# The last twelve blocks' out-projection as seven products a pair of blocks

## The chip, the cores and the metric

One core of a Trainium2 chip runs the kernel. Its engines work side by side, each through a list of instructions of its own, and wait for each other by semaphores: TensorE (PE in the profile) multiplies matrices from SBUF into the eight banks of PSUM; VectorE (DVE), ScalarE (ACT) and GpSimd (POOL) do elementwise work; SyncE (SP) issues most transfers between the chip's memory and SBUF. The metric is device time in microseconds (us) for one execution, lower is better.

## What is computed

```python
# linear attention with decay, 4 batches x 8 heads x 768 positions x 64, in blocks
intra = (qb @ kb.T * Dmask) @ vb
inter = (qb * lam_pow) @ kv_state
out   = intra + inter
kv_state = lam_block * kv_state + (kb * rev_pow).T @ vb
# then a feed-forward layer on x = out as (3072, 512)
h = x @ w_in            # (3072, 512) @ (512, 2048)
g = h * cos(h)
return g @ w_out        # (3072, 2048) @ (2048, 512)
```

Inputs and output are fp32; the matrix products work on bf16 copies and add up in fp32.

## The kernel before

The 3072 tokens are 24 blocks of 128. Attention goes by pairs of blocks (`pr`, 0 to 11): load q, k and v, prepare them (scale and cast, on GpSimd except early on), transpose q and k (by a DMA on SP's queue from pair 3 on), scores, state update, values. Its result, transposed, is `xT`.

The feed-forward layer goes by tiles, `TILES`, of two or four blocks. For each of the 16 slices `f` of 128 of the 2048 hidden columns TensorE multiplies `xT` by `w_in` into one PSUM bank (`ps_h`, four matmuls, line 753), ScalarE takes the cosine (`cos`, line 759), and VectorE multiplies the two into `g` in bf16 (line 765; "gate" below). Then, block by block, 16 matmuls over the slices add up g @ w_out into one bank (`ps_f`, line 800), with 512 columns of `w_out_sb` each. ScalarE copies the bank to `o_sb` (line 816) and SP's queue stores it. A tile's out-projection is interleaved with the hidden layer of the next tile; the last tile's stands alone at the end. The very last block is cut into 384 and 128 columns.

The order of all this is not written out by hand. `Planner` holds a list of tasks, each with an engine, a duration, what it depends on and a priority, and numbers of buffers (`BUFS`) and of PSUM banks. It plays them through once at build time, and each engine's instructions are emitted in the order found. An engine works strictly in that order: one that waits holds up all that stands behind it.

Tiles 5, 6 and 7 of before are the last twelve blocks, 12 to 23.

Of the kernel before, what the change touches and what calls it, by code (L numbers as in the profile page):

```python
# [19 lines left out]
DMA_FROM = 6  # L20
TILES = [4, 2, 2, 2, 2, 4, 4, 4]
SPLIT = 5
# [22 lines left out]
class Task:  # L45


    def __init__(self, eng, dur, deps, emit, prio, get=None, lat=None, banks=0):
        self.eng, self.dur, self.deps, self.emit, self.prio = eng, dur, [d for d in deps if d], emit, prio
        self.get, self.banks, self.lat = get, banks, lat  # L50

        self.frees, self.bank_frees = None, None

        self.worth = 0.0
        self.many = False

        self.then = None
        self.bank = []
        self.start = self.end = None
        self.ins, self.clears, self.extra = None, [], []  # L60


class Planner:
# [14 lines left out]
    def order(self):  # L78
# [3 lines left out]
        only = {}  # L82
        todo = list(self.tasks)
        while todo:
            first = {}
            for t in todo:
# [5 lines left out]
                if t.banks:  # L92
# [61 lines left out]
def kernel(  # L154
# [85 lines left out]

    unit = [MM(n * P, 4 * KF) + MM(DM, KF * n) + ATT * n for n in TILES]
    begins = [sum(unit[:i]) for i in range(len(unit) + 1)]
# [173 lines left out]
    def add_scores(pr, part):  # L416
# [293 lines left out]
    def add_span_state(s_t, prio):  # L710
# [20 lines left out]
        Uo[1, 1] = pl.add("POOL", 0.61, [x], state_16, prio)  # L731
        u.bank_frees = [[x]]

    h_last, o_last = {}, {}
    hid, closing = [], None

    def add_ffn(i):
        nb, n0 = TILES[i], first[i]
        cols = nb * P
# [230 lines left out]
```

## Time and profile before

| | before |
|---|---|
| median of 3 runs | 202.44 us (202.31 to 202.58) |
| span of the profiled execution, first to last instruction | 200.7 us; its own time is given only as this span |
| TensorE busy | 192.9 us, 96% |
| VectorE, ScalarE, GpSimd busy | 112.1, 117.1, 64.9 us |
| granted TensorE clock | 1.000 |

How to read it: busy shares tell which engine has little slack; the chain of waits, followed back from the last instruction, tells whose work the span is made of. "Idle before, releaser" is how long an engine stood still ahead of an instruction and what ended that. Matmuls overlap in the array, so the mean length of one (379 ns for 512 columns) is longer than its share of a stream of them; the latter is what counts for time.

### The profile page before, as it was taken

How to read it: one execution, taken by the hardware profiler on the slowest of the kernel's cores; microseconds unless marked ns; L12 is line 12 of the kernel's file. 1: busy time of each engine (PE TensorE's matmuls, PEld its weight loads, DVE VectorE, ACT ScalarE, POOL GpSimd, SP SyncE). 2: the span in 40 equal slices, each digit the busy share in tenths (PEclk: the TensorE clock that was granted, in tenths of full speed). 3: DMA queues.
4: the chain of work that ended last, by engine and by line, in shares of the span. 5: the costliest groups of instructions: out<-in, count | busy, mean ns of one | idle time of the engine just before them, and what ended most of it. 6: DMA issues, size and time to landing. Idle time of an engine off the chain costs nothing.

```text
span 200.7 us, 5731 instructions
## 1 busy us (share of the span) xinstructions
PE 192.9 (96%) x2380; PEld 110.2 (55%) x2407; DVE 112.1 (56%) x211; ACT 117.1 (58%) x223; POOL 64.9 (32%) x86
## 2 busy tenths in 40 slices
PE   8899999999999999999999999999999999999993
PEld 2466444648758647858755454544445444444452
DVE  2978772448848816956745679565445453444001
ACT  5878771329769527939555878486356465344120
POOL 5893002284373645472636570006400000000000
DMA  5999999999899999998999997999611010111112
GB/s 163 303 191 202 205 196 239 289 221 177 203 218 214 184 241 201 214 213 184 191 207 220 245 206 183 318 314 223 162 56 54 3 52 6 49 52 52 52 63 97
DMA packets 96668, 34.46 MB, mean 172 GB/s; under 512 B 84738, under 2 KB 93186, under 8 KB 96642
## 3 DMA queue, kind: packets, MB, share of 16 engines
q1 hardware_dynamic: 89664, 29.83, 66.6%
q0 software_dynamic: 6832, 4.20, 14.5%
q8 instruction: 19, 0.31, 0.7%
q10 hardware_dynamic: 146, 0.07, 0.1%
q14 instruction: 7, 0.06, 0.1%
HBM read 27.26 MB, written 6.29 MB: 167 GB/s over the span
## 4 chain that ended last, share of the span: by engine, by line
PE 89%; DMA 6%; issue 1%; SPq 1%; POOL 1%; ACT 0%; POOLq 0%
PE ps_f L800 41%; PE ps_h L753 41%; DMA sp_f<-in_k_dram 3%; DMA w_in_sb<-in_moe_w_in_dram 3%; PE ps_o L491 2%; PE ps_o L523 2%; PE ps_kv L441 2%; PE ps_s L429 1%; SPq L260 1%; POOL k_sp L614 1%; PE ps_t L381 0%; PE ps_kv L718 0%; PE ps_x L491 0%; ACT o_sb L816 0%; POOLq L614 0%
## 5 line engine op out<-in xcount | busy, mean ns | idle before, releaser
L765 DVE TENSOR_TENSOR g<-ps_h,cos 128x256 bf16<-128x256 f32 (+1 forms) x133 | 70.6, 543 | 41.4 <-ACT cos L759 39.7
L800 PE MATMUL ps_f<-w_out_sb,g 128*128 128x512 bf16 (+2 forms) x380 | 87.6, 370 | 2.2 <-issue 1.6
L753 PE MATMUL ps_h<-xT,w_in_sb 128*128 128x256 bf16 (+1 forms) x525 | 88.8, 319 | 0.5 <-issue 0.2
L759 ACT ACTIVATE cos<-ps_h,halfpi 128x256 f32<-128x256 f32 (+1 forms) x133 | 72.0, 570 | 28.9 <-PE ps_h L753 28.3
L753 PEld LDWEIGHTS <-w_in_sb 128*128 128x128 bf16 x532 | 51.4, 98 | 32.9 <-DMA w_in_sb<-in_moe_w_in_dram 0.4
L800 PEld LDWEIGHTS <-g 128*128 128x128 bf16 x400 | 37.6, 98 | 40.4
L351 POOL TENSOR_TENSOR qk<-q_f,q_scale 128x512 bf16<-128x512 f32 x19 | 19.4, 1042 | 54.2 <-DMA q_f<-in_q_dram 54.2
L816 ACT COPY o_sb<-ps_f 128x512 f32<-128x512 f32 (+1 forms) x24 | 13.7, 574 | 22.6 <-PE ps_f L800 19.6
L359 POOL TENSOR_TENSOR v_s<-v_f,v_scale 128x512 bf16<-128x512 f32 x19 | 19.6, 1043 | 9.2 <-DMA v_f<-in_v_dram 5.4
L531 ACT CAST xT<-ps_o 128x512 bf16<-128x512 f32 x15 | 8.1, 589 | 13.6 <-PE ps_o L523 11.2
L434 DVE TENSOR_TENSOR s_m<-ps_s,mask 128x512 bf16<-128x512 f32 x20 | 12.9, 685 | 2.5 <-PE ps_s L429 2.0
L355 POOL CAST qk<-k_f 128x512 bf16<-128x512 f32 x18 | 11.0, 612 | 7.8 <-DMA k_f<-in_k_dram 7.8
L447 DVE TENSOR_TENSOR sum<-sum,ps_kv 128x512 f32<-128x512 f32 x15 | 10.2, 682 | 0.7
L451 ACT CAST S<-sum 128x512 bf16<-128x512 f32 x15 | 9.1, 618 | 1.0 <-DVE sum L447 0.9
L508 DVE COPY spare<-ps_o 1x1 f32<-1x1 f32 x8 | 1.2, 156 | 14.6 <-PE ps_o L491 14.6
L816 DVE COPY o_sb<-ps_f 128x384 f32<-128x384 f32 x1 | 0.6, 558 | 11.6 <-PE ps_f L800 11.6
L491 PEld LDWEIGHTS <-v_s 64*64 64x64 bf16 x320 | 4.2, 106 | 4.4 <-issue 4.0
L491 PE MATMUL ps_o<-s_m,v_s 64*64 64x64 bf16 x288 | 5.9, 197 | 0.0
L638 DVE TENSOR_TENSOR s_m_sp<-ps_s,mask_sp 128x512 bf16<-128x512 f32 x8 | 5.1, 685 | 1.3 <-PE ps_s L633 1.3
L892 PE MATMUL ps_idle<-const-float32-1.0 128*128 128x512 f32 (+1 forms) x6 | 4.8, 902 | 0.8 <-PEq L954 0.8
L523 PE MATMUL ps_o<-qkT,S 64*64 64x64 bf16 x304 | 5.0, 195 | 0.0
L441 PE MATMUL ps_kv<-v_s,qk 64*64 64x64 bf16 x288 | 4.8, 195 | 0.0
(77 smaller groups left out, 83.9 us busy)
## 6 DMA issues: line engine op xcount, KB each, us to landing
q_f<-in_q_dram SPq DMA_DIRECT2D x20, 256.0 KB, 3.9
k_f<-in_k_dram SPq DMA_DIRECT2D x20, 256.0 KB, 4.5
v_f<-in_v_dram SPq DMA_DIRECT2D x20, 256.0 KB, 4.5
out_dram<-o_sb SPq DMA_DIRECT2D x19, 256.0 KB, 2.8
w_out_sb<-in_moe_w_out_dram POOLq DMA_DIRECT2D x3, 512.0 KB, 13.6
sp_f<-in_q_dram SPq DMA_DIRECT2D x2, 512.0 KB, 4.9
sp_f<-in_k_dram SPq DMA_DIRECT2D x2, 512.0 KB, 5.4
w_in_sb<-in_moe_w_in_dram POOLq DMA_DIRECT2D x2, 512.0 KB, 9.1
```

The costliest lines, as they stand in the source:

```text
L351: return vec[e].tensor_mul(new_qk()[:, 0, :, s], live.pop(("q_f", 2 * pr + s)), q_scale[:, c, :].unsqueeze(2).to_broadcast([P, H, D]))
L355: return (nc.scalar.copy if early else nc.gpsimd.tensor_copy)(new_qk()[:, 1, :, s], live.pop(("k_f", 2 * pr + s)))
L359: return vec[e].tensor_mul(live["v_s", 2 * pr + s], live.pop(("v_f", 2 * pr + s)), v_scale[:, c, :].unsqueeze(2).to_broadcast([P, H, D]))
L434: return nc.vector.tensor_mul(t, live["s", pr][s], mask.unsqueeze(1).to_broadcast([P, H, D]))
L447: return nc.vector.tensor_add(new, live["sum", pr, 0] if half else live["sum", pr - 1, 1], live["kv", pr][half])
L451: return nc.scalar.copy(new_S(pr, half), live["sum", pr, half])
L491: yield lambda h=h: nc.tensor.matmul(o[halves[h % 2], h // 2], lhsT=live["v_s", n0 + s][m, h, :], rhs=live["s_m", n0 + s][m, h, :], start= ...
L753: return [nc.tensor.matmul(t[:, :n], lhsT=w_in_sb[:, kd, f * P:(f + 1) * P], rhs=live["xT", i][:, kd, at], start=(kd == 0), stop=(kd == KD ...
L759: nc.scalar.activation(c[:, :n], live["h", i, f, at.start][:, :n], AF.Sin, bias=halfpi)
L765: return nc.vector.tensor_mul(live["g", i][:, f, at], live.pop(("h", i, f, at.start))[:, :n], live.pop(("c", i, f, at.start))[:, :n])
L800: return [nc.tensor.matmul(live["f", i, j, piece][:, :width], lhsT=live["g", i][:, f, j * P:(j + 1) * P], rhs=w_out_sb[:, f, part], start= ...
L816: return (nc.scalar.copy if eng == "ACT" else nc.vector.tensor_copy)(o[:, :width], live["f", i, j, piece][:, :width])
```

## The change

A pair of blocks and the two halves of the 2048 hidden columns make `g` a matrix of two by two blocks, a11 to a22 (first index: block of the pair). `w_out` is cut likewise: b11 to b22 (first index: half of its rows; second: half of its 512 columns). Strassen's scheme takes seven products where the plain one takes eight:

- "5": (a11+a12) b22, "2": (a21+a22) b11, "1": (a11+a22)(b11+b22), "3": a11 (b12-b22), "4": a22 (b21-b11), "7": (a12-a22)(b21+b22), "6": (a21-a11)(b11+b12).

Each product is eight matmuls of 256 columns, in two groups `g` of four slices of rows. Three banks are taken by a pair: A for 5 and 2, B for 1, C for 3 and 4 and, added onto them later, 6 and 7 (the very last pair has a bank D as well). ScalarE copies A to `SA`; VectorE makes `E` = B - SA in two halves, `o1` = C + SA (two quarters of the result), and, once 7 and 6 have been added onto C, `o2` = C + E (the other two). Products 7 and 6 wait until o1 has read C.

The sums on g's side are VectorE's, five for each group of each tile: `cmb` for 5, 2 and 1, and in place in `g` for 7 and 6. The sums of `w_out` are made once: three on GpSimd, into three tiles that hold the first pairs' data until then ("wide"), each in four instructions placed behind the preparation of a v; two in place in `w_out_sb`, eight instructions of VectorE, after the last plain out-projection has read it.

```diff
-TILES = [4, 2, 2, 2, 2, 4, 4, 4]
+FAST = [5, 6, 7, 8]
+TILES = [4, 2, 2, 2, 2, 4, 2, 2, 4]
+WIDE = ["11+22", "12-22", "21-11"]
+ON = ["DDDDDDDDDD"] * 9
+SLOT = list(range(6, 18))
+WSUM = [("11+22", "POOL", 2, 70.0), ("12-22", "POOL", 2, 70.0), ("21-11", "POOL", 2, 70.0), ("21+22", "DVE", 2, 100.0), ("11+12", "DVE", 2, 100.0)]
+SEQ = [[(n, (g,)) for g, x in enumerate(("52341", "34521")) for n in x] + [(n, (0, 1)) for n in "76"], [(n, (0, 1)) for n in "5234176"]]
...
+                if t.lock:
+                    at = max(at, free.get("POOL", 0.0))
+                if t.eng == "POOL":
+                    at = max(at, locked)
...
-    BUFS = {"ld": 6, "qk": 3, "v_s": 6, "qkT": 3, "s_m": 4, "cos": 3, "o_sb": 3, "o_held": 12}
+    BUFS = {"ld": 4, "qk": 3, "v_s": 6, "qkT": 3, "s_m": 4, "cos": 3, "o_held": 13, "cmb": 6, "SA": 1, "E": 1}
...
+        def two(_, name, g, at, e):
+            f, z = slice(QF * g, QF * g + QF), slice(HF + QF * g, HF + QF * g + QF)
+            b = {"11": w_out_sb[:, f, low], "12": w_out_sb[:, f, high], "21": w_out_sb[:, z, low], "22": w_out_sb[:, z, high]}
+            v = nc.vector if e == "DVE" else nc.gpsimd
+            return (v.tensor_add if name[2] == "+" else v.tensor_sub)(place(name, g)[:, at], b[name[:2]][:, at], b[name[3:]][:, at])
...
+        slices = [[f] for x in range(HF) for f in (x, x + HF)] if nb == 4 else [[x, x + HF] for x in range(HF)]
...
+            def hidden(task, fs=fs):
+                t = live["h", i, fs[0]] = bank(task.bank[0], [P, len(fs), cols], F32, "ps_h")
...
+        def combine(_, name, g, e):
+            v = nc.vector if e == "DVE" else nc.gpsimd
+            a11, a12, a21, a22 = (side(x, y, g) for x in range(2) for y in range(2))
+            if name in "125":
+                c = live["cmb", i, name, g] = work.tile([P, QF, np_, P], BF16, tag="cmb", bufs=BUFS["cmb"], name="cmb")
+                return v.tensor_add(c, *{"5": (a11, a12), "2": (a21, a22), "1": (a11, a22)}[name])
+            if name == "7":
+                return v.tensor_sub(a12, a12, a22)
+            return v.tensor_sub(a21, a21, a11)
...
+                    def product(task, name=name, g=g, p=p, to=to, half=half, what=what, opens=opens):
+                        if opens:
+                            live["f", i, p, to] = bank(task.bank[0], [P, 2, HM], F32, "ps_f")
+                        t = live["f", i, p, to][:, half]
+                        return [nc.tensor.matmul(t, lhsT=left(name, f, p), rhs=right(what, f),
+                                                 start=(f % QF == 0 and opens is not None), stop=(f == HF - 1), skip_group_check=True)
+                                for f in range(QF * g, QF * g + QF)]
...
+                        return nc.scalar.copy(live["SA", i, p], live["f", i, p, "A"])
...
+                        return nc.vector.tensor_sub(live["E", i, p][:, half], live["f", i, p, "B"][:, 0], live["SA", i, p][:, 1 - half])
...
+                        return nc.vector.tensor_add(o, live["f", i, p, "C"], live["SA", i, p])
...
+                nc.sync.dma_start(out=out[rows(0), high], in_=o[:, 0])
+                nc.sync.dma_start(out=out[rows(1), low], in_=o[:, 1])
...
+                    return nc.vector.tensor_add(o, live["f", i, p, "C"], e)
...
     def add_ffn(i):
+        if i in FAST:
+            return add_fast_ffn(i)
```

Up to the last plain out-projection (block 11) the order on TensorE, VectorE and ScalarE is as before. Below, lines are those of each kernel; old 765 is new 829 (gate), old 434 and 447 are new 452 and 465 (masked scores, state addition), old 508 is new 526 (a small marker copy). New are 776 (w_out sums), 850 (`cmb`), 852 and 853 (7 and 6 in place), 921 (E), 931 and 932 (o1), 958 and 959 (o2).

VectorE from the first gate of tile 5 on, before:

```order
L765 TENSOR_TENSOR g<-ps_h,cos 128x512 x9
L508 COPY spare<-ps_o 1x1
L765 TENSOR_TENSOR g<-ps_h,cos 128x512 x2
L434 TENSOR_TENSOR s_m<-ps_s,mask 128x512 x2
L447 TENSOR_TENSOR sum_2788<-sum_2502,ps_kv 128x512
L765 TENSOR_TENSOR g<-ps_h,cos 128x512 x2
L447 TENSOR_TENSOR sum_2812<-sum_2788,ps_kv 128x512
```

and now, from the masked scores of that tile on:

```order
L452 TENSOR_TENSOR s_m<-ps_s,mask 128x512 x2
L850 TENSOR_TENSOR cmb<-g 128x1024
L829 TENSOR_TENSOR g<-ps_h,cos 128x512 x3
L850 TENSOR_TENSOR cmb<-g 128x1024
L829 TENSOR_TENSOR g<-ps_h,cos 128x512
L850 TENSOR_TENSOR cmb<-g 128x1024
L829 TENSOR_TENSOR g<-ps_h,cos 128x512
L852 TENSOR_TENSOR g<-g 128x8x128
L853 TENSOR_TENSOR g<-g 128x8x128
L829 TENSOR_TENSOR g<-ps_h,cos 128x2x256
L850 TENSOR_TENSOR cmb<-g 128x1024
L829 TENSOR_TENSOR g<-ps_h,cos 128x2x256
```

The sums of the first group stand between the tile's last gates, those of the second between the first gates of tile 6, and the two state additions have moved behind these and the first pair's o1 and E. Ahead of this piece the eight w_out sums (776) stand between the first eleven gates.

VectorE at the program's end, before:

```order
L434 TENSOR_TENSOR s_m<-ps_s,mask 128x512 x2
L447 TENSOR_TENSOR S_3342<-sum_3001,ps_kv 128x512
L765 TENSOR_TENSOR g<-ps_h,cos 128x512
L542 TENSOR_TENSOR xT<-ps_o,cross_3419 128x4x64
L542 TENSOR_TENSOR xT<-ps_o,cross_3425 128x4x64
L765 TENSOR_TENSOR g<-ps_h,cos 128x512 x16
L816 COPY o_sb<-ps_f 128x384
```

and now, from the last gates on:

```order
L829 TENSOR_TENSOR g<-ps_h,cos 128x512 x2
L850 TENSOR_TENSOR cmb<-g 128x1024 x3
L852 TENSOR_TENSOR g<-g 128x8x128
L853 TENSOR_TENSOR g<-g 128x8x128
L921 TENSOR_TENSOR E<-ps_f,SA 128x256 x2
L931 TENSOR_TENSOR o_sb<-ps_f,SA 128x512
L958 TENSOR_TENSOR o_sb<-ps_f,E 128x512
L932 TENSOR_TENSOR o_sb<-ps_f,SA 128x256 x2
L921 TENSOR_TENSOR E<-ps_f,SA 128x256 x2
L959 TENSOR_TENSOR o_sb<-ps_f,E 128x256 x2
```

Behind the last gate stand five sums of the second group, and then both pairs' E, o1 and o2; the last one ends the program with its store.

GpSimd in two pairs' preparation (351, 355, 359 are q, k, v; new 369, 373, 377), before:

```order
L351 TENSOR_TENSOR qk<-q_f,q_scale 128x8x64 x2
L355 CAST qk<-k_f 128x8x64 x2
L359 TENSOR_TENSOR v_s<-v_f,v_scale 128x512 x2
L351 TENSOR_TENSOR qk<-q_f,q_scale 128x8x64 x2
L355 CAST qk<-k_f 128x8x64 x2
L359 TENSOR_TENSOR v_s<-v_f,v_scale 128x512 x2
```

and now:

```order
L369 TENSOR_TENSOR qk<-q_f,q_scale 128x8x64 x2
L373 CAST qk<-k_f 128x8x64 x2
L377 TENSOR_TENSOR v_s<-v_f,v_scale 128x512
L776 TENSOR_TENSOR w_12-22_1486<-w_out_sb 128x512
L377 TENSOR_TENSOR v_s<-v_f,v_scale 128x512
L776 TENSOR_TENSOR w_12-22_1486<-w_out_sb 128x512
L369 TENSOR_TENSOR qk<-q_f,q_scale 128x8x64 x2
L373 CAST qk<-k_f 128x8x64 x2
```

A w_out sum now stands behind each v of six pairs, and so ahead of the next pair's q.

More of the change, by code (lines that the diff above doesn't have):

```diff
@@ L109, in order @@
             free[t.eng] = t.end
+            if t.lock:
+                locked = t.end
             only.pop(t.eng, None)
@@ L239 @@
     live = {}
-    unit = [MM(n * P, 4 * KF) + MM(DM, KF * n) + ATT * n for n in TILES]
+    HF, HM = KF // 2, DM // 2
+    QF = HF // 2
+    unit = [MM(n * P, 4 * KF) + (MM(HM, 7 * HF * n // 2) if i in FAST else MM(DM, KF * n)) + ATT * n for i, n in enumerate(TILES)]
     begins = [sum(unit[:i]) for i in range(len(unit) + 1)]
@@ L455, in add_scores @@
         for s in range(2):
-            So[n0 + s] = pl.add("DVE", 0.69, [s_t] + ([So[n0]] if s else []), partial(scores_out, s=s), pa(0.25 + 0.1 * s), get="s_m")
+            So[n0 + s] = pl.add("DVE", 0.69, [s_t] + ([So[n0]] if s else []), partial(scores_out, s=s), pa(0.25 + 0.1 * s) - (HASTE if pr >= 8 else 0.0), get="s_m")
         s_t.bank_frees = [[So[n0]], [So[n0 + 1]]]
@@ L597 @@
     spans, span_deps = [], []
-    span_v = [consts.tile([P, H, 2, D], BF16, name=f"v_sp{x}") for x in range(SPANS)]
+    span_s = [consts.tile([P, 2, NP, 2, P], BF16, tag="wide", bufs=3, name=f"s_m_sp{x}") for x in range(SPANS)]
+    span_vs = consts.tile([P, SPANS, H, 2, D], BF16, tag="wide", bufs=3, name="v_sp")
+    span_v = [span_vs[:, x] for x in range(SPANS)]
     def add_span(x):
@@ L732, in add_span_state, with add_w_sums, place @@
         u.bank_frees = [[x]]
+        wide_free.append(u)
     h_last, o_last = {}, {}
     hid, closing = [], None
+    W, w_sum, passed, closed = {}, {}, {}, [None]
+    low, high = slice(0, HM), slice(HM, DM)
+    DUR = {"gate": (0.6, 0.17), "cos": (0.59, 0.16), "copy": (0.47, 0.18), "half": (0.34, 0.17)}
+    def add_w_sums():
+        def place(name, g):
+            if name in WIDE:
+                if name not in W:
+                    W[name] = consts.tile([P, HF, HM], BF16, tag="wide", bufs=3, name=f"w_{name}")
+                return W[name][:, QF * g:QF * g + QF]
+            return w_out_sb[:, QF * g:QF * g + QF, high] if name == "11+12" else w_out_sb[:, HF + QF * g:HF + QF * g + QF, low]
+        def two(_, name, g, at, e):
[3 more added lines that the diff above has]
+            return (v.tensor_add if name[2] == "+" else v.tensor_sub)(place(name, g)[:, at], b[name[:2]][:, at], b[name[3:]][:, at])
+        slots = []
+        for k, (name, e, parts, prio) in enumerate(WSUM):
+            for g in range(2):
+                loaded = [w_t["out", 0], w_t["out", 2]] if g == 0 else [w_t["out", 1]] + w_last
+                w_sum[name, g] = []
+                for x in range(parts):
+                    at = slice(x * QF // parts, (x + 1) * QF // parts)
+                    slot = [d_t[SLOT[len(slots)]]] if len(slots) < len(SLOT) else []
+                    slots.append(1)
+                    t = pl.add(e, {"DVE": 0.07 + 0.55 / parts, "POOL": 2.08 / parts}[e], loaded + slot + (wide_free if name in WIDE else [closed[0]] + w_sum[{"11+12": "12-22", "21+22": "21-11"}[name], g]),
+                               partial(two, name=name, g=g, at=at, e=e), prio + k + 0.4 * g + 0.01 * x)
+                    t.lock = e == "DVE"
+                    w_sum[name, g].append(t)
@@ L785, in add_ffn @@
             last = n0 + j == NBLK - 1
-            tag = "o_held" if n0 + j < len(HELD) or i == len(TILES) - 1 else "o_sb"
+            tag = "o_held"
             cuts = [0, 3 * DM // 4, DM] if last else [0, DM]
```

152 lines of the change are left out of this document (150 added, 2 removed).

## The prediction, made before the changed kernel ran

> **What bounds the kernel now.** I read the page's head and chain first, then busy time by stage, the chain in order of time, the groups by shape, and the timelines of VectorE, GpSimd and the SP queue where the change puts work.
>
> ```profile
> span 200.7 us, 5731 instructions
> PE 192.9 (96%) x2380; PEld 110.2 (55%) x2407; DVE 112.1 (56%) x211; ACT 117.1 (58%) x223; POOL 64.9 (32%) x86
> PE 89%; DMA 6%; issue 1%; SPq 1%; POOL 1%; ACT 0%; POOLq 0%
> ```
>
> TensorE is the chain. The stages that change begin with the hidden layer of tile 5 (blocks 12 to 15), at 109.7 us. In the stages below (columns: stretch, length, then busy us and count of each engine, granted clock, DMA share, GB/s) the clock is full and TensorE is idle for 0.8 of 74.3 us, so what TensorE no longer does comes off the span, unless another engine makes it wait.
>
> ```profile
> 109.50:125.00 15.50, 15.39 (x192) 7.66 (x193) 11.93 (x20) 12.72 (x21) 6.57 (x8) 1.00 1.04 206
> 125.00:131.50 6.50, 6.34 (x153) 3.47 (x152) 3.92 (x8) 3.37 (x6) 0.00 (x0) 1.00 0.94 314
> 131.50:159.60 28.10, 27.68 (x294) 13.39 (x297) 14.07 (x23) 15.78 (x27) 5.31 (x6) 1.00 0.49 130
> 159.60:183.80 24.20, 24.09 (x111) 10.96 (x112) 10.38 (x15) 12.65 (x20) 0.00 (x0) 1.00 0.09 33
> ...
> 183.80:200.70 16.90, 13.76 (x79) 7.05 (x78) 1.25 (x2) 2.71 (x5) 0.00 (x0) 1.00 0.21 79
> ```
>
> VectorE, the third busy time, is 40.3 us there and almost idle after 183.8. It takes nearly all of the new work.
>
> **TensorE's work.** The chain in order of time gives the price of one matmul in a stream (start, length, what):
>
> ```profile
> 77.68 6.99 PE ps_h L753 x64
> 101.34 5.18 PE ps_f L800 x24
> 190.50 7.12 PE ps_f L800 x48
> 197.65 0.27 ACT o_sb L816
> ```
>
> The 64 of the first row are 256 columns wide: 109 ns each. The 24 of the second are 512 wide: 216 ns. In the third, 16 are 512 wide (3.45) and the last block's 16 of 384 and 16 of 128 take the other 3.67.
> - Removed: 11 blocks x 16 x 0.216 + 3.67 = 41.65 us of out-projection.
> - Added: 6 pairs x 7 products x 8 = 336 matmuls of 256 columns, each with its own weights as in the first row: 336 x 0.1092 = 36.69. Gain 4.96.
> - The split of the third last tile turns 64 matmuls of 512 into 128 of 256 in its hidden layer: 13.98 for 13.81, a loss of 0.17. Cosine and gate still work on 512 columns, since two slices share a bank, so their number stays.
>
> TensorE does 4.79 us less.
>
> **VectorE's prices.** Groups by shape, then pieces of its timeline (start, length, count, idle before):
>
> ```profile
> L765 DVE TENSOR_TENSOR g<-ps_h,cos 128x512 bf16<-128x512 f32 x59 | 40.5, 691 | 31.7 <-ACT cos L759 31.2
> L765 DVE TENSOR_TENSOR g<-ps_h,cos 128x256 bf16<-128x256 f32 x74 | 30.3, 424 | 9.8 <-ACT cos L759 8.5 <-DMA v_f<-in_v_dram 0.7
> L384 DVE COPY qkT<-ps_t 128x1024 bf16<-128x1024 bf16 x2 | 1.4, 692 | 3.3 <-PE ps_t L381 3.3
> ```
> ```profile
> 107.11 1.29 DVE L434 TENSOR_TENSOR s_m<-ps_s,mask 128x512 bf16<-128x512 f32 x2
> 117.34 0.69 DVE L765 TENSOR_TENSOR g<-ps_h,cos 128x512 bf16<-128x512 f32 x1 [0.17 <-ACT cos L759]
> 58.42 0.76 DVE L542 TENSOR_TENSOR xT<-ps_o,cross 128x256 bf16<-128x256 f32 x2 [1.33 <-ACT cross L548]
> ```
>
> (The last row's shape is that of the 424 ns form.) An instruction of 512 fp32 elements lasts 0.69, but two in a row end after 1.29: one costs 0.60 when work waits. Two of 256 end after 0.76: 0.34 each. Adding a PSUM product to an SBUF tile has these forms, so a pair's E (two halves), o1 and o2 cost 2 x 0.34 + 2 x 0.60 = 1.9; six pairs 11.3.
>
> Sums of bf16 with both inputs in SBUF don't occur in the trace. From the slope of the first two rows (267 ns for 256 elements), 1024 elements would last 0.691 + 2 x 0.267 = 1.23 at one element a step; the COPY moves 1024 bf16 elements in 0.692. I take the COPY's, the only row with the type and the number of elements: 0.60 in a stream for 1024 (tiles of four blocks), 0.34 for 512 (tiles of two, and the w_out sums); 1.13 and 0.60 are the other end. Added: 20 x 0.60 + 20 x 0.34 + 8 x 0.34 = 21.5. [...]
>
> In all 32.8 us join VectorE's 40.3, in a stretch of some 86: not the bound as a whole, but it can be late in places. I walked its new order against TensorE's there.
>
> *Hidden layer of tile 5.* VectorE idles 15.50 - 11.93 = 3.6 us, mostly in gaps of 0.17 ahead of a gate. Eight w_out sums (2.7) fit if they run at once. GpSimd reads SBUF meanwhile:
>
> ```profile
> 113.88 2.04 POOL L351 TENSOR_TENSOR qk<-q_f,q_scale 128x512 bf16<-128x512 f32 x2 [2.21 <-DMA q_f<-in_q_dram]
> 118.18 2.07 POOL L359 TENSOR_TENSOR v_s<-v_f,v_scale 128x512 bf16<-128x512 f32 x2 [0.39 <-DMA v_f<-in_v_dram]
> 136.22 2.04 POOL L351 TENSOR_TENSOR qk<-q_f,q_scale 128x512 bf16<-128x512 f32 x2 [15.97 <-DMA q_f<-in_q_dram]
> ```
>
> About five of the sums fall into 113.9 to 120.3. Whether they and GpSimd hold each other up no row shows: from nothing to five times its 1.04 us. I take half an instruction each, 2.6 us of VectorE, of which its gaps absorb most; at the attention pair (118.7 on), where banks of late gates are wanted, TensorE waits 0.4.
>
> *Tile 5's products.* Behind the gates come three sums, the last gates, 7 and 6, then the second half's five, with tile 6's gates between. By my walk the second half's 5 and 2 are done at 130.2 and 131.4; TensorE, at the old pace, wants them at 130.7 and 131.1. With the semaphore: 0.5. The two state additions (old L447), moved behind E and o1, have until the next attention pair, some 13 us on, and cost nothing; if they came later, that pair would wait for them and their cast, about 1.2 (two forms of 0.6).
>
> *Last tile.* Its start today (the out-projection's first matmul, the last cosine, the last gate):
>
> ```profile
> 183.60 14.02 PE L800 MATMUL ps_f<-w_out_sb,g 128*128 128x512 bf16 x79
> 183.80 0.69 ACT L759 ACTIVATE cos<-ps_h,halfpi 128x512 f32<-128x512 f32 x1 [0.28 <-PE ps_h L753]
> 184.52 0.69 DVE L765 TENSOR_TENSOR g<-ps_h,cos 128x512 bf16<-128x512 f32 x1 [1.03 <-ACT cos L759]
> ```
>
> The last gate ends 1.6 us after the last hidden matmul. Then five sums, E and o1 of its first pair (8 instructions, 4.3 us in a stream) must be done when TensorE gets to product 7 of that pair, 6.1 on: level at 0.60 each, 0.6 late at 0.69. I take 0.3.
>
> Waits together 1.2, with ends of 0 and, if single rate or blocking holds, some 7.
>
> **Other parts.** *End.* The last copy (0.27) becomes an addition of the 0.42 form, +0.15. Its store grows from 64 to 128 KB:
>
> ```profile
> out_dram<-o_sb SPq DMA_DIRECT2D x1, 192.0 KB, 1.9
> out_dram<-o_sb ACTq DMA_DIRECT2D x1, 64.0 KB, 1.6
> ```
>
> Between these, +0.15. Together +0.3 (0.15 to 0.45).
>
> *GpSimd's twelve sums* of 512 elements go two to a pair of blocks, ahead of the next pair's q. The nearest two-input row:
>
> ```profile
> L359 POOL TENSOR_TENSOR v_s<-v_f,v_scale 128x512 bf16<-128x512 f32 x19 | 19.6, 1043 | 9.2 <-DMA v_f<-in_v_dram 5.4 <-PE ps_h L753 2.4 <-PE ps_kv L441 0.9
> 79.73 1.04 POOL L359 TENSOR_TENSOR v_s<-v_f,v_scale 128x512 bf16<-128x512 f32 x1 [1.01 <-DMA v_f<-in_v_dram]
> 83.75 2.05 POOL L351 TENSOR_TENSOR qk<-q_f,q_scale 128x512 bf16<-128x512 f32 x2 [2.98 <-DMA q_f<-in_q_dram]
> ```
>
> 2.09 us go into a wait of 2.98 for the load of q: free. At 1.5 us or more each, the excess delays the next transposes on the SP queue and all loads behind them; without that cover, 2.1 a pair.
>
> *SP queue.* Up to the first store of tile 5 its order is unchanged. Four load buffers instead of six add no wait there: each pair's loads already stand behind transposes that wait for a later preparation. But loads of the last pair of blocks now stand among tile 5's stores:
>
> ```profile
> 131.41 1.72 SPq L260 DMA_DIRECT2D q_f<-in_q_dram  x2
> 133.18 2.90 SPq L260 DMA_DIRECT2D k_f<-in_k_dram  x2
> 140.50 2.68 SPq L387 DMA_TRANSPOSE qkT<-qk  x2
> 153.28 0.43 PE L429 MATMUL ps_s<-qkT 64*64 64x64 bf16 x32
> ```
>
> k goes from 133.2 to about 137.5, behind o2 of tile 5's first pair, and the transposes from 140.5 to about 145. The scores that need them come at 153: 6 us of cover; beyond it each us costs one. Each pair stores four pieces of 128 KB for two of 256, on a queue with little else left: free.
>
> *ScalarE* loses these copies and gains six of the form:
>
> ```profile
> L816 ACT COPY o_sb<-ps_f 128x512 f32<-128x512 f32 x12 | 7.0, 586 | 12.8 <-PE ps_f L800 9.8 <-remote 2.9
> ```
>
> It idles ahead of them today, so nothing is gained or lost. *PSUM*: a pair holds three banks where a block held one, so a late VectorE is felt sooner; this is in the 1.2.
>
> **Sum.** -4.96 + 0.17 + 1.2 + 0.3 = -3.3. The profiled execution spans 200.7, so 197.4 of span; the runs' median lies 1.74 above it (202.44), and I keep that: **199.1 us**. Case range 198.4 to 200.4 (waits of 0.5 to 2.5).
>
> **Rivals.**
> 1. *VectorE is never late:* no waits, the gain less the end: 202.44 - 4.79 + 0.3 = 198.0. For it: VectorE's gaps in every stage above. Against it: my walk, late at two places by tenths.
> 2. *VectorE's sums and GpSimd's reads exclude each other.* If a sum waits out a whole GpSimd instruction, the five cost 5.2 us, with a gate behind each; pair 11's preparation (136.2 on) hits tile 5's sums again. Beyond the gaps TensorE loses some 3 instead of 1.2: 201. [...]
> 3. *Slower: bf16 sums run at one element a step.* 20 x 0.53 + 28 x 0.26 = 18 us more of VectorE. In tile 5's products it then has 8 gates (4.8), attention (2.6), ten sums (11.3) and two pairs (3.7), 22.4, plus some 4 left over, against 21 of TensorE: 5 late; at the end 2.5 more. Waits 7.5: 205.4. It decides from waits of 4.5 on, a long sum of about 0.88 us in a stream. For it: every two-input row of the trace has that rate (all fp32); against it: the COPY.
>
> **Chances.** Forecast 0.55, rival 1 0.15, rival 2 0.15, rival 3 and what else delays TensorE by over 4.5 us 0.15. Range 197.7 (rival 1 with the shortest end and today's gaps gone) to 202.0 (rival 2's upper part), leaving out rival 3 and a little. A change of 0.2% (0.4 us) is about what this measurement can tell from none. Faster 0.82, same 0.04, slower 0.14.
>
> **What would show it.** Out-projection at 109 ns a matmul, 336 of them; 1024-element sums of 0.69 and 512-element ones near 0.42; TensorE idle about 1.2 us more than now, put down to VectorE, at tile 5's products and at the last tile; GpSimd's sums of 1.04 ending before q lands; the chain up to 109.7 as before. Wrong would be sums of 1.2, or stretched ones beside GpSimd; matmuls above 0.109; waits of the last attention pair for its transposes.

## The result and the profile after

Four runs of the changed kernel took 200.6 us in the median (199.5 to 200.86), the kernel before 202.51 beside them: a ratio of 0.990, 95% interval 0.987 to 0.992. It is faster by 1.9 us where 3.3 were forecast. The profiled execution took 200.86 us with a span of 199.2. Medians and ranges are of fast runs; one slow run of the kernel with 60 idle matmuls (203.53) and three of the kernel without the split are left out of theirs.

The head of its page, busy time, and the chain by engine:

```profile
span 199.2 us, 6216 instructions
PE 190.0 (95%) x2577; PEld 130.1 (65%) x2599; DVE 146.3 (73%) x284; ACT 113.7 (57%) x217; POOL 79.3 (40%) x98
PE 87%; DVE 7%; DMA 2%; issue 2%; ACT 1%; DVEq 0%
```

TensorE is still the chain, but VectorE, which had no part in it, now holds 7%, and "issue" went from 1% to 2%. The stages of before, from tile 5's first gates on (columns as in the prediction):

```profile
109.50:125.00 15.50, 14.46 (x188) 7.17 (x189) 14.74 (x25) 11.53 (x18) 7.37 (x8) 1.00 1.14 185
125.00:131.50 6.50, 6.50 (x59) 5.50 (x57) 6.50 (x12) 2.85 (x5) 0.00 (x0) 1.00 0.79 221
131.50:159.60 28.10, 26.34 (x454) 23.04 (x453) 24.62 (x48) 13.75 (x23) 6.12 (x6) 1.00 0.66 167
159.60:183.80 24.20, 24.04 (x215) 15.41 (x217) 20.91 (x41) 13.67 (x24) 0.00 (x0) 1.00 0.10 34
183.80:199.20 15.40, 12.16 (x112) 10.62 (x109) 8.74 (x17) 1.80 (x3) 0.00 (x0) 0.99 0.25 87
```

TensorE, idle for 0.8 us of the first four stretches before, is idle for 3.0 of them now. VectorE has hardly a gap up to 131.5. These are TensorE's four longest waits there, from its timeline (in brackets the idle time ahead of the row and what ended it):

```profile
121.19 4.49 PE L820 MATMUL ps_h<-xT,w_in_sb 128*128 128x512 bf16 x19 [0.93 <-DVE g L829]
132.20 0.61 PE L897 MATMUL ps_f<-w_out_sb,cmb 128*128 128x256 bf16 x4 [0.41 <-DVE cmb L850]
141.66 0.22 PE L541 MATMUL ps_o<-qkT,S 64*64 64x64 bf16 x2 [1.04 <-issue]
157.21 0.35 PE L459 MATMUL ps_kv<-v_s,qk 64*64 64x64 bf16 x11 [0.31 <-ACT SA L914]
```

The first is the hidden layer after tile 5's attention, waiting for a bank that a late gate holds. The second is the second half of product 2. The third stands inside an attention visit (the block of attention matmuls of one pair), 30 of its last 32 matmuls done, and no semaphore explains it. The fourth waits for a copy to SA that stands behind a cosine on ScalarE. The new instructions' groups (the last number is the mean in ns):

```profile
L850 DVE TENSOR_TENSOR cmb<-g 128x1024 bf16<-128x1024 bf16 x12 | 8.7, 753 | 0.1
L850 DVE TENSOR_TENSOR cmb<-g 128x512 bf16<-128x512 bf16 x12 | 5.2, 455 | 0.1
L776 DVE TENSOR_TENSOR w_out_sb<-w_out_sb 128x512 bf16<-128x512 bf16 x8 | 4.9, 634 | 0.0
L776 POOL TENSOR_TENSOR w_11+22_953<-w_out_sb 128x512 bf16<-128x512 bf16 x4 | 4.6, 1155 | 0.0
```

The same shape, 128x512, has a mean of 455 ns in one place and 634 in another. VectorE's and GpSimd's timelines show why:

```profile
114.57 0.41 DVE L776 TENSOR_TENSOR w_out_sb<-w_out_sb 128x512 bf16<-128x512 bf16 x1
119.35 1.05 DVE L776 TENSOR_TENSOR w_out_sb<-w_out_sb 128x512 bf16<-128x512 bf16 x1
120.44 1.29 DVE L829 TENSOR_TENSOR g<-ps_h,cos 128x512 bf16<-128x512 f32 x2
122.84 1.50 DVE L850 TENSOR_TENSOR cmb<-g 128x1024 bf16<-128x1024 bf16 x1
```
```profile
119.08 1.04 POOL L377 TENSOR_TENSOR v_s<-v_f,v_scale 128x512 bf16<-128x512 f32 x1 [0.15 <-POOL qk L373]
122.75 1.04 POOL L377 TENSOR_TENSOR v_s<-v_f,v_scale 128x512 bf16<-128x512 f32 x1 [2.63 <-DMA v_f<-in_v_dram]
```

A w_out sum takes 0.41 alone. The one that starts at 119.35, in the middle of GpSimd's v (119.08 to 120.12), ends at 120.40, 0.28 after GpSimd's end. The gate behind it ends at 121.13, and TensorE goes on at 121.19. The first sum of g, 0.68 elsewhere, does the same at 122.84 and ends 0.55 after GpSimd's v.

To compare kernels I divide the span at weight loads, all of which are in the trace (some matmul records are missing): what lies ahead of tile 5's first weights; then the time from each weight load to the next, summed over the feed-forward layer and over attention; and what follows the last one.

| us | before | changed | changed, again | quiet GpSimd | half on GpSimd | the same, again |
|---|---|---|---|---|---|---|
| ahead of tile 5 | 109.30 | 108.98 | 109.28 | 109.45 | 109.18 | 109.27 |
| feed-forward from there | 83.45 | 79.35 | 78.76 | 78.76 | 78.83 | 79.31 |
| attention from there | 4.59 | 7.25 | 6.93 | 5.81 | 5.42 | 6.38 |
| behind the last weights | 3.4 | 3.6 | 3.5 | 3.6 | 3.6 | 3.7 |
| span | 200.7 | 199.2 | 198.5 | 197.6 | 197.0 | 198.6 |

(The last four columns are experiments below.) The feed-forward layer gives 4.1 to 4.7 us, as forecast; attention, in which the change adds no work, takes 0.8 to 2.7 of it back.

### The profile page after: what moved, and what is told of

It is laid out like the page before. It is cut to its first block, busy times and chain, and to the rows that moved or that the text cites. A ratio compares the mean times of both kernels' runs of the same rounds, so it can differ in the third digit from the quotient of the medians.

```text
span 199.2 us, 6216 instructions
## 1 busy us (share of the span) xinstructions
PE 190.0 (95%) x2577; PEld 130.1 (65%) x2599; DVE 146.3 (73%) x284; ACT 113.7 (57%) x217; POOL 79.3 (40%) x98
## 4 chain that ended last, share of the span: by engine, by line
PE 87%; DVE 7%; DMA 2%; issue 2%; ACT 1%; DVEq 0%
PE ps_h L1001 21%; PE ps_f L1048 21%; PE ps_h L820 17%; PE ps_f L897 17%; DVE g L829 3%; DMA sp_f<-in_q_dram 2%; DVE cmb L850 2%; PE ps_o L509 2%; PE ps_t L642 1%; PE ps_o L541 1%; PE ps_kv L459 1%; PE ps_s L447 1%; PE ps_s L653 1%; PE ps_o L679 1%; PE ps_idle L1143 1%
## 5 line engine op out<-in xcount | busy, mean ns | idle before, releaser
L826 ACT ACTIVATE cos<-ps_h,halfpi 128x512 f32<-128x512 f32 x48 | 32.9, 688 | 26.4 <-PE ps_h L820 24.9
L1013 DVE TENSOR_TENSOR g<-ps_h,cos 128x256 bf16<-128x256 f32 (+1 forms) x85 | 37.8, 459 | 12.2 <-ACT cos L1007 10.8
L1048 PE MATMUL ps_f<-w_out_sb,g 128*128 128x512 bf16 x177 | 42.3, 379 | 1.7 <-issue 1.3
L1007 ACT ACTIVATE cos<-ps_h,halfpi 128x256 f32<-128x256 f32 (+1 forms) x85 | 39.1, 505 | 7.1 <-PE ps_h L1001 6.9
L829 DVE TENSOR_TENSOR g<-ps_h,cos 128x512 bf16<-128x512 f32 x48 | 32.1, 685 | 5.3 <-ACT cos L826 5.2
L897 PEld LDWEIGHTS <-cmb 128*128 128x128 bf16 x144 | 14.0, 98 | 3.8 <-DVE cmb L850 0.7
L850 DVE TENSOR_TENSOR cmb<-g 128x1024 bf16<-128x1024 bf16 (+1 forms) x24 | 13.9, 604 | 0.2
L897 PE MATMUL ps_f<-w_out_sb,cmb 128*128 128x256 bf16 x96 | 13.3, 273 | 0.4 <-DVE cmb L850 0.4
L897 PE MATMUL ps_f<-w_out_sb,g 128*128 128x256 bf16 x96 | 12.4, 273 | 0.0
L1065 ACT COPY o_sb<-ps_f 128x512 f32<-128x512 f32 x12 | 6.9, 588 | 6.9 <-PE ps_f L1048 6.9
```

Of the source, the lines that this page charges most:

```text
L826: return nc.scalar.activation(c, live["h", i, fs[0]], AF.Sin, bias=halfpi)
L829: return nc.vector.tensor_mul(g_tile()[:, fs[0]:fs[-1] + 1:HF, :cols], live.pop(("h", i, fs[0])), live.pop(("c", i, fs[0])))
L850: return v.tensor_add(c, *{"5": (a11, a12), "2": (a21, a22), "1": (a11, a22)}[name])
L897: return [nc.tensor.matmul(t, lhsT=left(name, f, p), rhs=right(what, f), start=(f % QF == 0 and opens is not None), stop=(f == HF - 1), sk ...
L1007: nc.scalar.activation(c[:, :n], live["h", i, f, at.start][:, :n], AF.Sin, bias=halfpi)
L1013: return nc.vector.tensor_mul(live["g", i][:, f, at], live.pop(("h", i, f, at.start))[:, :n], live.pop(("c", i, f, at.start))[:, :n])
```

## The experiments

Theories: A, the wait of 1.04 is TensorE's own code coming late, where a visit of attention runs through a block of it faster than the next one is ready; D, VectorE's two-input sums and GpSimd's reads exclude each other. Such blocks are in the trace's records (page, queue q8: 20 loads of 16 KB in the changed kernel). From the first load to the last TensorE starts 4667 recorded instructions, 246 a load; some records are missing, and I take 256 for a block, my estimate. Rivals stand with each expectation.

**The changed kernel again** (no edit).

> The changed kernel once more, unedited. In its profile TensorE waits three times from 109 us on: 0.93 us at 121.2 behind a gate, 0.41 at 132.2 behind a sum of g, and 1.04 at 141.7 that no semaphore explains. Theory A (the 1.04 is the load of TensorE's next 256 instructions, which comes too late because the instruction count puts the boundary into an attention visit): the count is fixed, so the stall stands at 141.7 again, 0.8 to 1.3 us, in the same place after 30 of the visit's last 32 matmuls. Rival B (a chance delay of that one execution): it is gone or elsewhere. Both: median 199.5 to 201.

200.37 us (199.87 to 201.32; ratio 0.990, 0.987 to 0.993). TensorE's waits in its profile:

```profile
120.47 0.44 PE L459 MATMUL ps_kv<-v_s,qk 64*64 64x64 bf16 x31 [0.78 <-DVE g L829]
121.84 4.49 PE L820 MATMUL ps_h<-xT,w_in_sb 128*128 128x512 bf16 x19 [0.38 <-DVE g L829]
141.04 0.22 PE L541 MATMUL ps_o<-qkT,S 64*64 64x64 bf16 x2 [0.35 <-issue]
```

The stall stands ahead of the very same matmul, but is a third as long: a fixed place, a varying size. The wait for product 2 is gone. The waits near 121 are 1.16 instead of 0.93.

**The boundary moved away.**

```diff
-    ones_of(4 * P, F32)
+    for _ in range(32):
+        ones_of(64)
```

> One idle fp32 matmul at the start is replaced by 32 idle matmuls of 64 columns: 63 more instructions on TensorE's queue ahead of everything, in time in which TensorE idles (3.3 to 5.4 us); all work after it and its order unchanged. Theory A: every boundary of 256 instructions moves 63 instructions forward. Counted on the trace of the changed kernel, the fastest 256 instructions between two boundaries now last 3.35 us (to 88.1 us) instead of 1.66, and the load needs about 2.7 from boundary to boundary: no stall anywhere, 1.0 us less, 199.4 to 199.9. Rival B or C (the stall belongs to that visit of attention, whatever stands ahead): 1.04 at 141.7 stays and the time is the changed kernel's within 0.3.

200.48 us (199.28 to 201.31). In the profile the visit runs through without a gap (its last group, the next product; no idle time in brackets):

```profile
140.68 0.48 PE L541 MATMUL ps_o<-qkT,S 64*64 64x64 bf16 x32
141.09 1.05 PE L897 MATMUL ps_f<-w_12-22_1517,g 128*128 128x256 bf16 x8
```

The stall went, the time didn't fall: this profile waits 0.87 and 0.48 near 121 and began tile 5 0.4 us later than the control. The forecast of 1.0 us less was a miss: a stall of 0.24 to 0.62, as most profiles have it, is lost in the spread of four runs. The idle matmuls may also cost at the start what they save here. All six kernels that have them begin tile 5 at 109.64 to 110.49, those without at 108.98 to 109.45, but for one at 110.59, which waits 1.5 for the load of w_in; the two effects are not separated.

**The boundary moved onto another visit, twice.** With 60 idle matmuls of 32 columns:

> The same with 60 idle matmuls of 32 columns, 119 more instructions. Theory A: the fastest 256 instructions between boundaries are then those that end at 107.3 us, 1.52 us by the trace, so the stall leaves 141.7 and comes back as about 1.2 us near 107.3, in the attention ahead of tile 5, a place where the kernel before and the changed one have no wait; time as the changed kernel's, within 0.4. Rivals B and C: nothing at 107.3, 1.04 at 141.7 as ever.

200.86 us (199.72 to 202.12). No stall at 141, and none at 107 either: half a miss. I had counted boundaries on the trace, where records are missing. Counted in TensorE's instruction list, the stall had stood ahead of number 4036 = 16 x 256 - 60 in every profile of the unpadded kernel, and 60 matmuls had put a boundary eight instructions too late. So 65 of them:

> The second try at placing the stall. 65 idle matmuls of 32 columns, 126 instructions more. The boundary is now taken from the program itself: the stall stood ahead of instruction 4036 in three profiles, and 4036 is 256 x 16 - 60, so boundaries lie at 256 n - 60. With 60 matmuls the boundary lay 8 instructions behind the start of the visit near 107 us, and the next one four wide matmuls behind its end, late enough for the load; with 65 it lies two ahead of the visit's start and two ahead of its end. Theory A: a stall of 0.1 to 0.9 us near 107.5 to 108.5, ahead of the last matmul of that visit's last 32, and none at 141.7. Rival C: nothing there. Time as the changed kernel's, within 0.5.

201.34 us (200.77 to 201.66). The visit near 107:

```profile
107.74 0.50 PE L541 MATMUL ps_o<-qkT,S 64*64 64x64 bf16 x31
108.65 0.21 PE L541 MATMUL ps_o<-qkT,S 64*64 64x64 bf16 x1 [0.41 <-issue]
```

A stall of 0.41, ahead of the last of 32, in a visit that had none above 0.2 in any other profile; its instruction is number 3268 = 13 x 256 - 60, three blocks of 256 ahead of 4036. The trace's records of instruction loads (16 KB each) show the block in question landing at 107.35, 1.3 us before TensorE goes on; in the six profiles with the stall at 4036 that distance is 1.28 to 1.47. The place is the one that theory A gave, and the kernel without the split, below, stalls at a third such place. The landing does not itself end the stall: in the changed kernel's profile the block landed at 140.22 and TensorE went on at 141.66. What fills that time no record shows. The kernel before has the same visits and no stall; that its count put the boundaries elsewhere fits, but was not tested.

**GpSimd quiet.** Its preparations for pairs 8 to 11 compute one head of eight (here q; k and v likewise):

```diff
+            if pr >= 8:
+                to, src = new_qk()[:, 0, :, s], live.pop(("q_f", 2 * pr + s))
+                nc.gpsimd.memset(to[:, 1:], 0.01)
+                return nc.gpsimd.tensor_mul(to[:, :1], src[:, :1], q_scale[:, c, :1].unsqueeze(2).to_broadcast([P, 1, D]))
```

> GpSimd's preparations of q, k and v for pairs 8 to 11 work on one head of eight; the other seven heads are filled with a constant (these values are left out). GpSimd still waits for the same loads, but reads an eighth and is done early. VectorE's work and order are untouched. Theory D (a VectorE sum with both inputs in SBUF stands still while GpSimd reads SBUF): the w_out sums of 1.05 to 1.5 us fall to 0.41, those of 128x512 in tile 5's stage from a mean of 634 ns to under 450, and the 0.93 wait at 121.2 falls to 0.3 or less; 0.6 to 1.0 us less. The 0.41 at 132.2 shrinks or goes too. Rival E (VectorE is late there by the sheer number of its instructions): sums keep their time or the wait stays above 0.7; no gain. The stall at 141.7 stays by theory A, since TensorE's count is the same.

199.24 us (199.02 to 199.67; ratio 0.984, 0.983 to 0.986), 1.1 less than the control of the same chip. The w_out sums as a group, and the two waits that are left near 121 and 140 (line numbers are shifted by the edit):

```profile
L788 DVE TENSOR_TENSOR w_out_sb<-w_out_sb 128x512 bf16<-128x512 bf16 x8 | 3.2, 417 | 0.0
```
```profile
121.03 4.49 PE L832 MATMUL ps_h<-xT,w_in_sb 128*128 128x512 bf16 x19 [0.42 <-DVE g L841]
140.11 0.22 PE L553 MATMUL ps_o<-qkT,S 64*64 64x64 bf16 x2 [0.24 <-issue]
```

634 ns became 417, and of 0.9 to 1.2 near 121 0.42 remains, which is the length of the one w_out sum that stands between the visit and the gates. Product 2's wait is absent, as in the control. Theory D holds; E, the sheer number of instructions, is the smaller part. The runs also lie within 0.65 us of each other, against 1.45 of the control. GpSimd's instructions start when loads land (one pair's v at 119.08 and 122.75 in the first profile of the changed kernel, from 116.97 on in the second), so which sums meet them changes from one execution to the next. Beside GpSimd's memset, which has no input, a sum keeps its 0.41 (118.19 to 118.60, inside 118.18 to 118.65); those that were held up stood beside its multiplications, casts and sums.

**The w_out sums made tiny.**

```diff
+            ... (*(x[:, at, :8 if e == "DVE" else HM] for x in (place(name, g), b[name[:2]], b[name[3:]])))
```

> The eight in-place w_out sums on VectorE take 8 of 256 columns (the rest is left out), 16 elements instead of 512; they stay where they are in VectorE's order, and GpSimd's work is whole. Theory D in its strict form (the one that comes second stands still until the other's instruction ends): most last under 0.1 us, but each that starts during a GpSimd instruction lasts to the end of it, some up to 1 us, and a wait of TensorE of 0.1 to 0.6 remains at tile 5's attention in some executions. Rival G (the two share a rate, and each slows in proportion to what it moves): no tiny sum over 0.25 us, no wait left. Both: 199.2 to 200.0.

199.61 us (199.09 to 200.56; 0.986, 0.983 to 0.989). Two pieces of GpSimd's and VectorE's timelines:

```profile
115.53 0.62 POOL L373 CAST qk<-k_f 128x512 bf16<-128x512 f32 x1 [0.18 <-DMA k_f<-in_k_dram]
118.44 1.04 POOL L377 TENSOR_TENSOR v_s<-v_f,v_scale 128x512 bf16<-128x512 f32 x1 [0.78 <-DMA v_f<-in_v_dram]
```
```profile
115.79 0.37 DVE L776 TENSOR_TENSOR w_out_sb<-w_out_sb 128x16 bf16<-128x16 bf16 x1
118.38 0.16 DVE L776 TENSOR_TENSOR w_out_sb<-w_out_sb 128x16 bf16<-128x16 bf16 x1
119.24 0.34 DVE L776 TENSOR_TENSOR w_out_sb<-w_out_sb 128x16 bf16<-128x16 bf16 x2
```

A sum of 16 elements lasts 0.16 alone. The one that starts inside the cast (115.53 to 116.15) ends at 116.16: it stood still to the end, though it had almost nothing to read. The first of the two at 119.24 ends at 119.50, with GpSimd's v (118.44 to 119.48). That is against G, a shared rate. TensorE's wait near 121 was 0.16, at the low end of what was expected.

The full-sized sums say the same in every profile. 54 of them, of 512 elements, begin during a multiplication, cast or sum of GpSimd, from 0.03 to 1.17 us after its start and with more than 0.13 us of it left. Wherever they begin, all end 0.27 or 0.28 us after GpSimd's instruction. Those of 1024 end 0.55 after one. A sum that shared a rate would end at differing distances.

**All eight sums to GpSimd, by the planner.**

```diff
-... ("21+22", "DVE", 2, 100.0), ("11+12", "DVE", 2, 100.0)]
+... ("21+22", "POOL", 2, 100.0), ("11+12", "POOL", 2, 100.0)]
```

> The two in-place sums of w_out, eight instructions, go from VectorE to GpSimd, where they stand ahead of the preparation of v of the next pair. 22 idle matmuls at the start in place of one (40 instructions more on TensorE) keep every boundary of 256 at least 30 instructions away from the start of a visit of attention, so that theory A expects no stall. Theory D (VectorE's sums and GpSimd's reads exclude each other): with no two-input sum among tile 5's gates, TensorE's waits there, 0.4 to 1.3 us in the four profiles so far, fall to 0.2 or less, and the runs lie closer together: 199.0 to 199.6, with GpSimd busy for some 9 us more at 1.15 each. Rival F (the exclusion only moves): GpSimd's v, pushed back to 122 to 126 us, now meets VectorE's sums of g; these stretch to 1 to 1.5 us and TensorE waits 0.4 to 1.0 at tile 5's products instead: 199.8 to 200.6.

203.93 us (202.52 to 204.95; 1.007, 1.004 to 1.010): no faster than the kernel before, a miss for both theories. (The edit also puts 22 idle matmuls at the start.) The planner, given other costs, found another order for TensorE too. It waits at tile 5's second attention, moved up, for masked scores that now stand behind E and gates on VectorE:

```profile
136.57 0.19 PE L447 MATMUL ps_s<-qkT 64*64 64x64 bf16 x1 [1.05 <-DVE E L921]
137.16 0.44 PE L447 MATMUL ps_s<-qkT 64*64 64x64 bf16 x31 [0.41 <-DVE g L829]
138.37 0.21 PE L459 MATMUL ps_kv<-v_s,qk 64*64 64x64 bf16 x1 [0.76 <-DVE g L829]
138.96 0.44 PE L459 MATMUL ps_kv<-v_s,qk 64*64 64x64 bf16 x31 [0.38 <-DVE s_m L452]
```

These are 2.6 us. They are not the whole loss. Right behind them the granted clock is 0.50 for 3.4 us, from 139.8 to 143.2. The products there, and the clock in 40 slices of the span:

```profile
139.75 3.59 PE L897 MATMUL ps_f<-w_out_sb,g 128*128 128x256 bf16 x16
PEclk9999999999999999999999999997899999999999
```

The same 16 matmuls take 1.91 in the changed kernel, so this costs 1.7 more. Eight of the nine runs have this profile's mean clock, 0.992; the ninth, at 1.000, took 202.52, the time of the kernel before. The wait near 121, which the edit was for, is gone; since the order differs too, the run says nothing more about it.

**All eight to GpSimd, order unchanged.** Only the engine that emits is changed, and the idle matmuls of the second run are kept (its 200.48 is the control).

```diff
-            v = nc.vector if e == "DVE" else nc.gpsimd
+            v = nc.gpsimd
```

> The eight in-place w_out sums go from VectorE to GpSimd again, but this time at the very places of the order that they have in the changed kernel, so that the orders of TensorE, ScalarE and the SP queue are those of the kernel with 32 idle matmuls (its control, 200.48); e5 had also given TensorE another order. By e5's profile one such sum takes GpSimd 1.12 us and tile 5's hidden layer then has no wait. Theory D: the waits at the attention near 121 (0.87 and 0.48 in the control's profile) go to 0.2 or less. GpSimd, idle for some 8 us in that stretch, takes 9.0 us more, so its last preparations come about 3 us later, to 126 or 127, and its reads run beside VectorE's sums of g: 0 to 1 us of new wait at tile 5's products. In sum 199.2 to 200.0. Rival F (the exclusion moves whole): as the control, 200.2 to 201. Rival E (the waits near 121 are a matter of VectorE's own backlog from attention): they stay above 0.5.

200.21 us (199.34 to 200.45). No wait near 121, but the first sum of g now meets GpSimd's v, pushed back to 122.4, and both halves of product 2 wait:

```profile
122.95 2.08 DVE L850 TENSOR_TENSOR cmb<-g 128x1024 bf16<-128x1024 bf16 x1
```
```profile
127.48 0.61 PE L897 MATMUL ps_f<-w_out_sb,cmb 128*128 128x256 bf16 x4 [0.38 <-DVE cmb L850]
132.88 0.61 PE L897 MATMUL ps_f<-w_out_sb,cmb 128*128 128x256 bf16 x4 [0.43 <-DVE cmb L850]
```

Between D and F, and by the time nearer to F: most of the gain moves elsewhere.

**Half of them.** With and, as the single edit against the changed kernel, without the idle matmuls:

```diff
-            v = nc.vector if e == "DVE" else nc.gpsimd
+            v = nc.gpsimd if e == "POOL" or name == "11+12" else nc.vector
```

> As the run before, but only four of the eight sums (those of product 6, wanted last) go to GpSimd; four stay on VectorE. Theory D: VectorE's remaining four all come ahead of GpSimd's last v, so at most one meets it; the waits near 121 fall to 0.4 or less, and GpSimd's 4.5 us fit into its idle time with a delay of about 1 us. 199.2 to 199.8. Rival F: 200.2 or more.

> The run before (four of the eight in-place sums on GpSimd, 199.49) without its idle matmuls: the single edit against the changed kernel. Theory A: the stall of TensorE ahead of instruction 4036 is back at about 141, 0.2 to 1.3 us; with the waits near 121 gone as there, 199.6 to 200.4. If the idle matmuls cost as much at the start as they save here (their kernels began tile 5 0.3 to 0.7 us later), the time is that of the run before within 0.2.

> The run before once more, in five rounds, for its interval against the kernel before. If its gain over the changed kernel is real (0.990 of the kernel before): 0.983 to 0.987, and an upper end of the interval under 0.988. If it was the luck of four runs: 0.988 to 0.991. In the profile no wait above 0.3 near 121, the stall ahead of instruction 4036 again.

With them 199.49 us (199.15 to 199.82; 0.985, 0.983 to 0.987); without, 199.38 (198.73 to 200.04; 0.985, 0.983 to 0.987) and, again, 199.68 (198.98 to 200.31; 0.986, 0.983 to 0.988). None of the three profiles has a wait above 0.2 near 121. The stall at 4036 is there in both profiles without idle matmuls and gone with them; the time doesn't tell these apart. The two profiles without, first sum of g, then TensorE's waits:

```profile
122.06 0.68 DVE L850 TENSOR_TENSOR cmb<-g 128x1024 bf16<-128x1024 bf16 x1
```
```profile
139.51 0.22 PE L541 MATMUL ps_o<-qkT,S 64*64 64x64 bf16 x2 [0.24 <-issue]
```
```profile
122.04 1.46 DVE L850 TENSOR_TENSOR cmb<-g 128x1024 bf16<-128x1024 bf16 x1
```
```profile
131.41 0.61 PE L897 MATMUL ps_f<-w_out_sb,cmb 128*128 128x256 bf16 x4 [0.37 <-DVE cmb L850]
141.03 0.22 PE L541 MATMUL ps_o<-qkT,S 64*64 64x64 bf16 x2 [1.19 <-issue]
```

One kernel, spans of 197.0 and 198.6: 0.95 is the stall's size and 0.37 product 2's wait, which comes when that first sum meets GpSimd (1.46 to 2.08 in four profiles) and not when it doesn't (0.68). This kernel, about 1 us ahead of the changed one and 3 of the one before, is the fastest found that computes everything. Its gain over the changed kernel is likely rather than certain: the repeat's interval ends at 0.9882, just above the 0.988 set for it, and the changed kernel's begins at 0.987.

**No split of the third last tile.**

```diff
-FAST = [5, 6, 7, 8]
-TILES = [4, 2, 2, 2, 2, 4, 2, 2, 4]
+FAST = [5, 6, 7]
+TILES = [4, 2, 2, 2, 2, 4, 4, 4]
```

> The third last tile is not split: tiles of 4, 4 and 4 blocks at the end, all three by the seven products. The hidden layer of the blocks 16 to 19 goes back from 128 matmuls of 256 columns to 64 of 512, 0.17 us less by the prediction's term; the sums of g are then ten of 1024 elements in a tile instead of twenty of 512, 6.8 us instead of 8.4 of VectorE, but all behind the gates of a larger tile. If the split costs only its matmuls: 0.2 less, 199.8 to 200.4. If it is what keeps TensorE supplied between tiles: waits of 0.5 to 2 us at the products of tile 6, 200.8 to 202.

201.19 us in the median of the seven runs with a clock of 1.000 (200.44 to 203.05; ratio 0.994, 0.991 to 0.997). The other three have a mean clock of 0.992 and took 205.14 to 206.17. The profile is of one of these, and shows what made it long:

```profile
133.55 0.48 PE L541 MATMUL ps_o<-qkT,S 64*64 64x64 bf16 x19 [3.10 <-issue]
PEclk9999999999999999999999999969999999999999
```

A stall of 3.10 stands ahead of the 14th of the visit's last 32 matmuls, which is number 3780 = 15 x 256 - 60 of TensorE's list, and its block landed at 132.02, 1.53 before TensorE goes on. That is late code once more. Behind it the clock is 0.50 from 132.9 to 136.3. The boundary one block earlier lies 37 instructions ahead of the visit, where the other stalls have two or four. The load of the late block began only at 131.10, when TensorE had already stopped; why so late stays open. Ahead of the visit TensorE also waits 0.91 for a sum of g. So the time, in the second of the expected ranges, is no clean measure of the split: late code at a new place is mixed in, and how much of it the other seven runs have is not recorded.

## Why the prediction was right or wrong

- **TensorE's work, -4.79: right.** Where no sum is late, the feed-forward layer falls from 83.45 to 78.76, by 4.69. The last 112 matmuls of products are 12.28 in the chain, 109 ns each. The split's 0.17 is inside this; its own price wasn't measured.
- **VectorE's prices: right.** 1024 elements of bf16 last 0.68 wherever GpSimd is quiet, 512 0.41. Rival 3, one element a step, is out.
- **The last tile, 0.3: wrong,** there is no wait, by a margin of 0.05: its o1 ends at 189.64 and TensorE goes on with the products 7 and 6 at 189.69.
- **The end, +0.3: the term came to about 0.2** (3.4 us behind the last weights became 3.5 to 3.7).
- **ScalarE at nothing: wrong by 0.31,** the copy to SA that comes behind a cosine, in nearly every profile.
- **GpSimd's twelve sums and the SP queue, at nothing: right.** The sums take 1.155 us each, tile 5 begins at 108.98 and 109.28 instead of 109.30, and no wait of TensorE behind that is put down to a transfer.
- **The waits in tile 5's hidden layer, 0.4: the step that failed.** The place and the mechanism were named, and the price of the meetings was no underestimate. VectorE lost 1.1 to 1.7 us to them over the eight sums in five profiles (means of 557 to 634 ns for 417) where 2.6 were priced. What failed is that "its gaps absorb most": the last of the eight stands between the visit and the gates whose bank TensorE wants, with no gap behind it. With GpSimd quiet TensorE waits 0.42 there, that sum's own length; a sum held to the end of GpSimd's instruction (1.05 to 1.25 us for 0.41) can come on top, and TensorE lost 0.4 to 1.35 in those five profiles. The blocking is that of rival 2. Its 201 had about 3 us of waits in all. With one to three of the eight sums held for most of an instruction, not five, and of tile 5's sums mainly the first, the waits for late gates and sums were 1.3 and 1.2 in the two profiles of the changed kernel. The 54 sums above waited for the rest of GpSimd's instruction; 91 gates, with one input in PSUM, that run inside an instruction of GpSimd keep 0.67 to 0.69.
- **Tile 5's products, 0.5: right in size (0.41) by luck, wrong in cause.** I had derived it from VectorE's backlog. It comes only where the first sum of g meets an instruction of GpSimd; the second profile of the changed kernel, in which it doesn't, has no such wait.
- **Not in the prediction at all:** TensorE's late code, 0.24 to 1.19 by the profiles of kernels with that instruction count.

The two profiled executions of the changed kernel (200.86 and 200.23) lie 1.8 and 1.1 us above the forecast. Their waits are 2.7 and 1.8 instead of 1.2, which is 1.5 and 0.6 of that. With GpSimd quiet they are 1.0, and the time, 199.24, is the forecast within 0.15. The median of 200.6 lies inside the stated range but above the forecast's own 198.4 to 200.4, close to rival 2's 201. That it comes so close is partly luck, since late code, which no rival had, makes 0.35 to 1.04 of the waits.

## What to carry to other kernels

Before an instruction with both inputs in SBUF goes to VectorE, look at GpSimd's row for the same stretch: price each meeting at the rest of GpSimd's instruction (here the 54 sums ended 0.27 or 0.28 us behind it), not a share, and look whether a gap follows it before another engine wants what stands behind. If sums are to be divided between the two, leave the planned order alone and move only as many as GpSimd's idle time holds. A gap put down to "issue" in a dense run of small matmuls, always at the same instruction, may be late code: look in the record of instruction loads for one that lands shortly before the engine goes on (1.28 to 1.53 us here). Its place depended here on the number of instructions ahead of it (63 more of them took the stall away from 141, 126 more brought one of 0.41 near 108), so a change far away can bring it or take it. When forecast and runs differ by an amount of the size of the runs' spread, take a second profile of the same kernel before explaining the first.

## What of the hardware was not expected

- TensorE's code was loaded in pieces of 16 KB, and the stalls stood ahead of numbers 3268, 3780 and 4036, which are 512 and 256 apart. Where nothing stalls, a visit of 256 small instructions took 1.37 to 1.50 us in the profiles of the kernel before and the changed one. From the boundary ahead of the visit that stalls to the use of the next block 2.1 and 2.8 us went by in the two profiles of the changed kernel. Visits that began two or four instructions behind a boundary stalled near their end, by 0.24 to 1.19 us in seven profiles. In one profile, with the boundary 37 instructions ahead of the visit and a load that began late, it was 3.10.
- A VectorE sum with both inputs in SBUF that began 0.03 us or more into a GpSimd multiplication, cast or sum, with more than 0.13 us of it left, did not end before it: 54 of 54 sums of 512 elements ended 0.27 or 0.28 us after it. The rest of one instruction is not always the end of it: once a sum of 1024, 0.68 alone, waited through two v in a row and took 2.08.
- Behind 2.6 us of waits within 3.4, and behind a stall of 3.10, the granted clock was 0.50 for 3.4 us; in the profiles of the other changed kernels, where no single wait is above 1.19, the mean clock is 0.999 or 1.000. That the idle time is the cause is not shown, but all eleven runs at a mean of 0.992 are of these two kernels.
- GpSimd is held up as well: a sum of w_out takes it 1.12 us in a row of its own, and 1.33 beside VectorE's sums; a q pair 2.04 alone and up to 2.53. In the changed kernel's profile two sums of VectorE that begin 0.01 and 0.02 us into an instruction of GpSimd keep 0.41 and 0.43, and GpSimd's two last 1.33 and 1.34 instead of 1.04.
- The kernel with half of the sums on GpSimd spanned 197.0 and 198.6 us in two profiles, both at a clock of 1.000; the late code and one sum held up by GpSimd are 1.3 of the 1.6.
